# Layer two's output products in the last two passes: seven block products of 256 columns for eight of a half

## Chip, cores and metric

One core of a Trainium2 chip runs one program. The metric is the time of one execution in microseconds; of several runs the median is given. TensorE (PE in the rows) multiplies, VectorE (DVE), ScalarE (ACT) and GpSimd (POOL) do the element-wise work, SyncE (SP) issues nearly all transfers.

## What is computed

```python
def reference(**kwargs):
    ...
    attn_out = _attn_ref(**attn_kwargs)                    # q, k, v: (4, 8, 576, 64)
    x = np.ascontiguousarray(attn_out.transpose(0, 2, 1, 3)).reshape(B * S, H * D)
    x = _moe_ref(x=x, **moe_kwargs)                        # 512 -> 1536, gated -> 512
    return _moe2_ref(x=x, **moe2_kwargs)

def _moe2_ref(x, w_in, w_out):
    h = x @ w_in                                           # 2304x512 @ 512x2048
    r = np.maximum(h, 0.0)
    g = r * r
    return (g @ w_out).astype(np.float32)                  # 2304x2048 @ 2048x512
```

A causal retention with a decay per head comes first, then layer one, then layer two. The weights arrive as 64-bit floats and are rounded to 32-bit ones on the chip.

## The kernel before

**Numbers.** Every float32 operand of layers one and two is split into a high half and a low half of type fp32r (`split`: ScalarE copies the high half, VectorE subtracts it for the low one), and a product is three matmuls: high by high, high by low, low by high (`three`).

**Passes and systems.** Layer two runs in three passes (2,0), (2,1), (2,2) of 768 tokens, each token set in two halves a and b of 384. A pass has 8 systems; system k makes the hidden columns of two blocks of 128, for a and b. A system's input product is a 2x2 block product done with seven multiplications and sums (`slot`, products 1 to 7): a slot is 6 matmuls of 384 columns, into banks named g (two of them), v (two) and z (one). Evictions go to the tiles ca* (a) and cb* (b): ScalarE copies, VectorE adds and squares (`scalar_tensor_tensor`, the square of the positive part). The sums of the weights are made once, in pass (2,0), by GpSimd (`stationary`), and read back from DRAM as `wi` in later passes; the sums of the activations are renewed at the passes' borders (`renew`: xo_h, xo_l).

**Output products.** When the two blocks of a system are squared, `hidden` splits them into ho_hi and ho_lo. After every second system, `out2` multiplies them: for each half (a, b) and each 128 tokens j = 0, 1, 2 it makes a tile of 128 tokens by 512 output columns, in 4 blocks x 3 = 12 matmuls of 512 columns, the stationary operand being the 128x128 block of hidden values, the moving one a block of 128x512 of `wo` (high and low, loaded from DRAM by `load_out`). The tile is accumulated in one of three banks `a1` to `a3` (`out_bank`, named oacc) and added to `xy` by VectorE (in a pass's first pair of systems ScalarE copies it); after the last pair it is written out. `xy` holds the layer's inputs and, in the place of those used up, its outputs.

**Order.** The loop at the end runs over systems n: `seq` lists the slots, 1 and 2 and 6 and 5 of system n between 7 and 4 and 3 of system n - 1, with the output tiles of earlier systems (`outs`) and the loads (`fetch`) placed between them. A scheduler then fixes each engine's order from a timeline of its own; each engine takes its instructions strictly in that order.

**Memory.** Pools are stacked: raw and converted weights (`raw_p`, `cv_p`), then `ho2_p` and `wo2_p` for the second layer; on the other side `wi_p`, `s1_p`, `xs_p`, `xo_p` and `c4_p` (the tiles ca*, cb*).

## Time and profile before

| | |
|---|---|
| median of 3 runs | 875.48 us (874.52 to 876.61) |
| the profiled execution, first to last instruction | 875.1 us |
| TensorE busy | 863.9 us (99%), 5064 matmuls |
| weight loads on TensorE (beside matmuls) | 746.0 us (85%) |
| VectorE / ScalarE / GpSimd busy | 642.8 (73%) / 400.9 (46%) / 122.2 us (14%) |
| granted TensorE clock | full in all 40 slices |
| transfers | 203.62 MB, 65.8% of the queues' time |

The profile is one execution, and its span is the time that the working is made against; what lies around the span in a run is not shown. Matmuls overlap one another, so their durations add up to more than the time they take; the distance from one start to the next is what counts. Pass (2,1) begins near 605 us with the first slot of 384 columns of its first system; the last input product ends near 855 us, and only output products follow.

### The profile page before, as it was taken

How to read it: one execution, taken by the hardware profiler on the slowest of the kernel's cores; microseconds unless marked ns; L12 is line 12 of the kernel's file. 1: busy time of each engine (PE TensorE's matmuls, PEld its weight loads, DVE VectorE, ACT ScalarE, POOL GpSimd, SP SyncE). 2: the span in 40 equal slices, each digit the busy share in tenths (PEclk: the TensorE clock that was granted, in tenths of full speed). 3: DMA queues.
4: the chain of work that ended last, by engine and by line, in shares of the span. 5: the costliest groups of instructions: out<-in, count | busy, mean ns of one | idle time of the engine just before them, and what ended most of it. 6: DMA issues, size and time to landing. Idle time of an engine off the chain costs nothing.

```text
span 875.1 us, 13516 instructions
## 1 busy us (share of the span) xinstructions
PE 863.9 (99%) x5064; PEld 746.0 (85%) x5064; DVE 642.8 (73%) x1002; ACT 400.9 (46%) x709; POOL 122.2 (14%) x135
## 2 busy tenths in 40 slices
PE   9989999999999999999999999999999999999998
PEld 7878888888888888888888899989899988998987
DVE  3899999998976899677647999999534467533544
ACT  3657777565544544644325466554233233232310
POOL 3343343223130010000002311120000000000000
PEclk9999999999999999999999999999999999999999
DMA  9994777755554489878745388988666465656412
GB/s 337 402 356 160 253 249 249 264 186 211 196 192 154 139 282 379 297 273 288 253 141 185 144 315 328 361 304 313 206 239 215 126 226 210 190 202 204 164 41 73
DMA packets 75218, 203.62 MB, mean 233 GB/s; under 512 B 7696, under 2 KB 18448, under 8 KB 75152
## 3 DMA queue, kind: packets, MB, share of 16 engines
q1 hardware_dynamic: 74720, 202.34, 65.8%
q8 instruction: 40, 0.66, 0.3%
q10 hardware_dynamic: 432, 0.41, 0.1%
q14 instruction: 26, 0.21, 0.1%
HBM read 138.23 MB, written 64.49 MB: 232 GB/s over the span
## 4 chain that ended last, share of the span: by engine, by line
PE 86%; DVE 7%; DMA 4%; issue 2%; ACT 1%; SPq 0%; POOL 0%; DVEq 0%; POOLq 0%; ACTq 0%
PE oacc L113 42%; PE g L113 24%; PE v L113 12%; PE z L113 6%; DVE w L113 3%; DMA qk_sb<-in_qk 3%; DVE wi L113 1%; PE o L113 1%; DMA k_sb<-in_kv 1%; DMA qs_sb<-in_qscale 1%; PE s L113 1%; DVE xy L113 1%; DVE cbg L113 0%; PE kv L113 0%; DVE xo_l L113 0%
## 5 line engine op out<-in xcount | busy, mean ns | idle before, releaser
L113 PE MATMUL g<-xo_h,wi 128*128 128x384 f32 (+1 forms) x768 | 238.3, 364 | 0.0
L113 PE MATMUL oacc<-wo,ho_hi 128*128 128x512 f32 (+1 forms) x584 | 179.5, 388 | 0.0
L113 PEld LDWEIGHTS g<-xo_h,wi 128*128 128x128 f32 x768 | 142.5, 188 | 17.1
L113 PE MATMUL oacc<-ho_hi,wo 128*128 128x512 f32 (+1 forms) x480 | 151.1, 370 | 0.5 <-ACT xy L113 0.5
L113 DVE TENSOR_TENSOR xy<-oacc,xy 128x512 f32<-128x512 f32 (+1 forms) x155 | 99.6, 648 | 59.6 <-PE oacc L113 59.1
L113 PE MATMUL g<-xo_l,wi 128*128 128x384 f32 (+1 forms) x384 | 139.6, 364 | 0.0
L113 PEld LDWEIGHTS oacc<-wo,ho_hi 128*128 128x128 f32 x584 | 108.4, 188 | 19.2
L113 PE MATMUL v<-xo_h,wi 128*128 128x512 f32 (+1 forms) x384 | 123.2, 364 | 0.0
L113 PE MATMUL oacc<-wo,ho_lo 128*128 128x512 f32 (+1 forms) x292 | 113.3, 390 | 0.0
L113 PEld LDWEIGHTS oacc<-ho_hi,wo 128*128 128x128 f32 x480 | 88.1, 188 | 17.6 <-ACT xy L113 1.3
L113 PE MATMUL oacc<-ho_lo,wo 128*128 128x512 f32 (+1 forms) x240 | 89.1, 371 | 0.0
L113 PEld LDWEIGHTS g<-xo_l,wi 128*128 128x128 f32 x384 | 72.1, 188 | 8.4
L113 DVE TENSOR_SCALAR w<-w 128x512 f32<-128x512 f32 (+1 forms) x136 | 64.9, 480 | 18.0 <-ACT w L113 17.0
L113 PEld LDWEIGHTS v<-xo_h,wi 128*128 128x128 f32 x384 | 71.2, 188 | 8.0
L113 DVE TENSOR_TENSOR cbg<-v,cbg 128x384 f32<-128x384 f32 (+1 forms) x72 | 43.1, 598 | 45.8 <-ACT cbg L113 24.3
L113 ACT ACTIVATE cag<-g 128x384 f32<-128x384 f32 (+1 forms) x36 | 19.0, 528 | 125.2 <-PE g L113 125.1
L113 PE MATMUL v<-xo_l,wi 128*128 128x512 f32 (+1 forms) x192 | 69.8, 363 | 0.0
L113 PEld LDWEIGHTS oacc<-wo,ho_lo 128*128 128x128 f32 x292 | 54.8, 188 | 11.2
L113 PE MATMUL z<-xo_h,wi 128*128 128x512 f32 (+1 forms) x192 | 62.5, 365 | 0.0
L113 ACT CAST ho_hi<-cbg 128x768 fp32r<-128x768 f32 (+1 forms) x36 | 32.7, 908 | 45.5 <-DVE cbg L113 44.4
L113 DVE SCALAR_TENSOR_TENSOR w<-raw,w 128x512 uint32<-128x512 uint32 x68 | 52.5, 773 | 0.7
L113 PEld LDWEIGHTS oacc<-ho_lo,wo 128*128 128x128 f32 x240 | 45.1, 188 | 8.7
(90 smaller groups left out, 1295.6 us busy)
## 6 DMA issues: line engine op xcount, KB each, us to landing
wi<-win SPq DMA_DIRECT2D x84, 512.0 KB, 4.2
raw<-in_w SPq DMA_DIRECT2D x68, 512.0 KB, 4.9
win<-wi SPq DMA_DIRECT2D x60, 512.0 KB, 3.6
wo<-wsp SPq DMA_DIRECT2D x44, 512.0 KB, 6.4
wsp<-wo SPq DMA_DIRECT2D x28, 512.0 KB, 5.2
qk_sb<-in_qk SPq DMA_DIRECT2D x15, 576.0 KB, 7.4
wst<-w SPq DMA_DIRECT2D x32, 256.0 KB, 6.0
wi<-win SPq DMA_DIRECT2D x28, 256.0 KB, 5.4
```

What stands on the lines that cost most here:

```text
L113: i = op(*args, **kw)
```

## The change

In passes (2,1) and (2,2) the output products of a pair of systems become 2x2 block products with seven multiplications. A block row is a 128-token tile of a or of b (same j), a block column one of the two hidden blocks of a system, and the output columns are taken in halves of 256. A product is then 2 systems x 3 = 6 matmuls of 256 columns (`out3`). Each token pair j has seven of them, accumulated in two banks: 1, 6, 7, 4 in one and 5, 3, 2 in the other, and most of them are added to `xy` between two products of the same bank.

The operands: `block_tiles` gives ca* and cb* (now caa, cab) for both systems of a pair at once, in two sets of buffers. `sums2` has GpSimd make four sums of blocks per token pair, in the part of `xy` that pass (2,0) has left; `prepare` splits the seven operands of a token pair with three copies of 512, 256 and 1024 columns on ScalarE and as many subtractions on VectorE (hs_h, hs_l, two buffers). For the weights, `sums` has GpSimd make four sums of the raw blocks per system in pass (2,1) (w_o), which `operand2` splits (wt) and stores (tsp); pass (2,2) loads them from there; the three unsummed blocks are loaded from wsp. `hidden`'s splits, `load_out` and `out2` remain for pass (2,0) only. The products are taken from `stream` at 1.5 per slot from slot 23 on (`flow`).

```diff
@@ -54,6 +54,10 @@
+PRODUCTS = (1, 5, 6, 3, 7, 2, 4)
+START = 2
@@ -652,7 +661,10 @@
-        if i == 1:
+        if i == 1 and n >= turn_over:
+            s["x"] = bank("g")[:, :m]
+            s["a"], s["b"] = block_tiles(n)
+        elif i == 1:
@@ -707,6 +719,8 @@
     def hidden(n, which, c):
+        if n >= turn_over:
+            return
@@ -763,23 +777,115 @@
+    def block_tiles(n):
+
+        k = systems[n][2]
+        if k % 2 == 0:
+            home = block_pools[k // 2 % 2]
+            pairs_of[n] = pairs_of[n + 1] = [
+                home.tile([P, 2, 2, M[2]], F32, tag=f"g{x}", name=f"ca{x}") for x in "ab"
+            ]
+        return [x[:, k % 2] for x in pairs_of[n]]
...
+    def sums(n):
+
+        w0, w1_ = raw_o[n]
+        b11, b12, b21, b22 = (w[:, a:a + 256] for w in (w0, w1_) for a in (0, 256))
+        for a, x, y, op in ((b22, b22, b12, ALU.subtract), (b12, b12, b11, ALU.subtract),
+                            (b11, b11, b22, ALU.add), (b21, b21, b11, ALU.subtract)):
+            pool_e.tensor_tensor(out=a, in0=x, in1=y, op=op)
+
+    def operand2(n, i):
+
+        ph, p, k, what = systems[n]
+        w = moving[n, i] = t_p.tile([P, 2, 256], F32R, tag=f"t{i}", name="wt")
+        if i in (1, 2, 3):
+            f, at = {1: (0, 0), 2: (1, 0), 3: (1, 256)}[i]
+            sp.dma_start(out=w.bitcast(F32), in_=wsp[2, "o", 2 * k + f][:, :, at:at + 256])
+            return
+        x = (6, 5, 4, 7).index(i)
+        if p == 1:
+            split(w[:, 0], w[:, 1], raw_o[n][x // 2][:, x % 2 * 256:][:, :256])
+            sp.dma_start(out=tsp[k][:, x], in_=w.bitcast(F32))
+        else:
+            sp.dma_start(out=w.bitcast(F32), in_=tsp[k][:, x])
...
+    def sums2(n, j):
+
+        a, b = (x[:, :, :, j * P:(j + 1) * P] for x in pairs_of[n])
+        a11, a12, a21, a22 = (x[:, :, f] for x in (a, b) for f in range(2))
+        sums_of[n, j] = s = xy[:, :, 2 * P * j:2 * P * (j + 1)].rearrange("p i (s q) -> p i s q", q=P)
+        for x, y, z, op in ((0, a21, a22, ALU.add), (2, a11, a21, ALU.subtract),
+                            (1, s[:, 0], a11, ALU.subtract), (3, a12, s[:, 1], ALU.subtract)):
+            pool_e.tensor_tensor(out=s[:, x], in0=y, in1=z, op=op)
+
+    def prepare(n, j):
+
+        a, b = (x[:, :, :, j * P:(j + 1) * P] for x in pairs_of[n])
+        hi, lo = (hl_p.tile([P, 7, 2, P], F32R, tag=x, name=f"hs_{x}") for x in "hl")
+        halves[n, j] = hi, lo
+        split(hi[:, 0:2], lo[:, 0:2], a.rearrange("p s f q -> p f s q"))
+        split(hi[:, 2], lo[:, 2], b[:, :, 1])
+        split(hi[:, 3:7], lo[:, 3:7], sums_of[n, j])
...
+    def out3(n, j, at):
+
+        ph, p, k, what = systems[n]
+        i = PRODUCTS[at]
+        if at < 2:
+            banks[j, at] = out_bank()
+        o = banks[j, at % 2 if at < 6 else 0]
+        o = o[:, 256:] if i == 2 else o[:, :256]
+        x = (1, 2, 4, 5, 6, 7, 3).index(i)
+        for s in range(2):
+            hi, lo = (z[:, x, s] for z in halves[n, j])
+            th, tl = (moving[n - 1 + s, i][:, y] for y in range(2))
+            for y, (c, d) in enumerate(((hi, th), (hi, tl), (lo, th))):
+                pe.matmul(
+                    o, c, d, start=i in (1, 5, 2) and s + y == 0, stop=s == 1 and y == 2, skip_group_check=True
+                )
...
+        if k == 1 and i in (1, 5, 6, 4):
+            act.copy(home, src)
+        else:
+            tt(out=home, in0=src, in1=home, op=ALU.add)
+        if k == F2 // 2 - 1 and i in (3, 7, 2, 4):
+            half = slice(256 * half, 256 * half + 256)
+            sp.dma_start(out=out[t0:t0 + P, half].rearrange("p (c q) -> p c q", q=P), in_=home)
@@ -869,9 +975,91 @@
+    def follow(n, j, at):
+        out3(n, j, at)
+        own = [m for m in (n + 2, n + 3) if m < end]
+        if j == 2:
+            for m in own:
+                operand2(m, PRODUCTS[at])
+        if at == 6:
+            flowed["out"] += 1
+            ready_halves()
...
+            slots["n"] += 1
+            flow(int(1.5 * (slots["n"] - begin_at)))
...
+            t_p, hl_p = pool(ctx, "t_p", 3), pool(ctx, "hl_p", 2)
```

The rest of the diff moves pools (those of the raw weights, `ho2_p` and `wo2_p` are closed in pass (2,1) to make room for `t_p`, `hl_p` and the second set of ca*, cb*) and splits the last loop at system `turn_over`, the first of pass (2,1).

**Where the order moves.** First TensorE, at the first pair of systems of pass (2,1), behind the third product (bank v) of its second system. Before, an output tile of pass (2,0) follows at once:

```order
L113 MATMUL v_6494<-xo_l_6355,wi_6352 128x384
L113 MATMUL v_6494<-xo_h_6354,wi_6352 128x384 x2
L113 MATMUL v_6494<-xo_l_6355,wi_6352 128x384
L113 MATMUL v_6494<-xo_h_6354,wi_6352 128x384
L113 MATMUL oacc_6601<-wo_6097,ho_hi_6217 128x512 x2
L113 MATMUL oacc_6601<-wo_6097,ho_lo_6218 128x512
L113 MATMUL oacc_6601<-wo_6102,ho_hi_6217 128x512 x2
L113 MATMUL oacc_6601<-wo_6102,ho_lo_6218 128x512
L113 MATMUL oacc_6601<-wo_6240,ho_hi_6348 128x512 x2
L113 MATMUL oacc_6601<-wo_6240,ho_lo_6349 128x512
L113 MATMUL oacc_6601<-wo_6245,ho_hi_6348 128x512 x2
L113 MATMUL oacc_6601<-wo_6245,ho_lo_6349 128x512
```

Now 18 matmuls of input products, 12 block products on the plain blocks (oacc_6770 and oacc_6883) and 18 more of input products follow; then stands the piece below, whose oacc rows are the first on sums (hs_h_6716 is token pair 0, hs_h_6724 token pair 1):

```order
L120 MATMUL v_6841<-xo_h_6239,wi_6677 128x384
L120 MATMUL v_6841<-xo_l_6240,wi_6677 128x384
L120 MATMUL v_6841<-xo_h_6239,wi_6677 128x384 x2
L120 MATMUL v_6841<-xo_l_6240,wi_6677 128x384
L120 MATMUL v_6841<-xo_h_6239,wi_6677 128x384
L120 MATMUL oacc_6786<-wt_6576,hs_h_6716 128x256 x2
L120 MATMUL oacc_6770<-wt_6580,hs_h_6716 128x256 x2
L120 MATMUL oacc_6883<-wt_6580,hs_h_6724 128x256 x2
L120 MATMUL oacc_6786<-wt_6576,hs_l_6717 128x256
L120 MATMUL oacc_6786<-wt_6598,hs_h_6716 128x256 x2
L120 MATMUL oacc_6786<-wt_6598,hs_l_6717 128x256
L120 MATMUL oacc_6770<-wt_6580,hs_l_6717 128x256
```

Between the last matmul of that third product and the first of oacc_6786 stand 36 matmuls of 384 columns and 12 of 256. Output products start here after a pause in which only input products run.

Second, GpSimd. Before, its queue ends with the sums of the input weights of pass (2,0):

```order
L113 TENSOR_TENSOR w_in_5611<-w_in_5611 128x256 [waits Pool_49]
L113 TENSOR_TENSOR s1_5978<-w_in_5779 128x256 [waits DMAHW1_49,DVE_49]
L113 TENSOR_TENSOR w_in_5779<-w_in_5778,w_in_5779 128x256 [waits DMAHW7_49,Pool_49]
L113 TENSOR_TENSOR w_in_5778<-s1_5978,w_in_5778 128x256 [waits DVE_49,Pool_49]
L113 TENSOR_TENSOR w_in_5778<-w_in_5778 128x256 [waits Pool_49]
```

Now the sums of the first pair of systems follow (`sums2`; caa_6364 and cab_6365 are its a and b, xy_78 takes the sums). The first two sums of each of the three token pairs come first, then the third ones, a sum of weights (w_o) and the fourth ones:

```order
L120 TENSOR_TENSOR xy_78<-cab_6365 128x256 [waits DMAHW5_49,DMAHW4_49,DVE_49]
L120 TENSOR_TENSOR xy_78<-caa_6364,cab_6365 128x256
L120 TENSOR_TENSOR xy_78<-cab_6365 128x256 [waits DMAHW6_49,DMAHW0_49]
L120 TENSOR_TENSOR xy_78<-caa_6364,cab_6365 128x256
L120 TENSOR_TENSOR xy_78<-cab_6365 128x256 [waits DMAHW6_49,DMAHW1_49]
L120 TENSOR_TENSOR xy_78<-caa_6364,cab_6365 128x256
L120 TENSOR_TENSOR xy_78<-xy_78,caa_6364 128x256 [waits Pool_49] x3
L120 TENSOR_TENSOR w_o_6619<-w_o_6619,w_o_6618 128x256 [waits DMAHW4_49,DMAHW3_49,Activation_49]
L120 TENSOR_TENSOR xy_78<-caa_6364,xy_78 128x256 [waits Pool_49] x3
```

ScalarE's copy hs_h_6716<-xy_78 of 1024 columns waits for the first of the last three, which is the eleventh instruction of this piece.

Third, VectorE near the end, where no input products are left. Before, low halves are done ahead of the evictions:

```order
L113 SCALAR_TENSOR_TENSOR cbg_8095<-cbg_8095 128x2x384 [waits DVE_49]
L113 TENSOR_TENSOR ho_lo_8235<-cag_8094,ho_hi_8234 128x768 [waits Activation_49]
L113 TENSOR_TENSOR ho_lo_8261<-cbg_8095,ho_hi_8260 128x768 [waits Activation_49]
L113 TENSOR_TENSOR xy_78<-oacc_8278,xy_78 128x4x128 [waits PE_49]
L113 TENSOR_TENSOR xy_78<-oacc_8293,xy_78 128x4x128 [waits PE_49]
L113 TENSOR_TENSOR xy_78<-oacc_8308,xy_78 128x4x128 [waits PE_49]
L113 TENSOR_TENSOR xy_78<-oacc_8323,xy_78 128x4x128 [waits PE_49]
L113 TENSOR_TENSOR xy_78<-oacc_8338,xy_78 128x4x128 [waits PE_49]
L113 TENSOR_TENSOR xy_78<-oacc_8353,xy_78 128x2x128 [waits PE_49]
L113 TENSOR_TENSOR xy_78<-oacc_8368,xy_78 128x2x128 [waits PE_49]
```

Now each token pair's three subtractions (hs_l) stand among the evictions of the pair ahead; one round of it:

```order
L120 TENSOR_TENSOR hs_l_9137<-caa_8713,hs_h_9136 128x512 [waits Activation_49]
L120 TENSOR_TENSOR xy_78<-oacc_9154,xy_78 128x2x128 [waits PE_49]
L120 TENSOR_TENSOR hs_l_9137<-cab_8714,hs_h_9136 128x256 [waits Activation_49]
L120 TENSOR_TENSOR xy_78<-oacc_9144,xy_78 128x2x128 [waits DVE_49,PE_49]
L120 TENSOR_TENSOR hs_l_9137<-xy_78,hs_h_9136 128x1024 [waits Activation_49]
L120 TENSOR_TENSOR xy_78<-oacc_9217,xy_78 128x2x128 [waits PE_49]
L120 TENSOR_TENSOR xy_78<-oacc_9154,xy_78 128x2x128 [waits PE_49]
L120 TENSOR_TENSOR xy_78<-oacc_9144,xy_78 128x2x128 [waits PE_49]
L120 TENSOR_TENSOR xy_78<-oacc_9217,xy_78 128x2x128 [waits PE_49]
L120 TENSOR_TENSOR xy_78<-oacc_9154,xy_78 128x2x128 [waits PE_49]
```

The subtraction of 1024 columns has moved in front of the eviction of oacc_9217, whose bank TensorE needs three products later.

## Rows read from the trace of the kernel before

**Rows 1.** the page, busy time, share of the span and instructions of each engine

```profile
PE 863.9 (99%) x5064; PEld 746.0 (85%) x5064; DVE 642.8 (73%) x1002; ACT 400.9 (46%) x709; POOL 122.2 (14%) x135
```

**Rows 2.** windows: busy us (instructions) by engine; then TensorE's granted clock, DMA share, GB/s

```profile
480.00:520.00 40.00, 40.00 (x201) 36.06 (x200) 37.90 (x55) 20.44 (x36) 12.70 (x12) 1.00 0.56 203
605.00:872.00 267.00, 266.86 (x1336) 239.77 (x1334) 130.24 (x189) 71.41 (x119) 0.00 (x0) 1.00 0.54 180
```

**Rows 3.** timeline of TensorE, pass (2,1): start us, us, engine, line, op out<-in, shape, count

```profile
639.99 0.34 PE L113 MATMUL v<-xo_h,wi 128*128 128x384 f32 x1
...
643.12 0.63 PE L113 MATMUL oacc<-wo,ho_hi 128*128 128x512 f32 x2
...
645.89 0.34 PE L113 MATMUL z<-xo_h,wi 128*128 128x384 f32 x1
```

**Rows 4.** chain that ended last: start, us, what, count; then timeline of TensorE, end

```profile
854.67 17.21 PE oacc L113 x87
...
863.84 0.39 PE L113 MATMUL oacc<-wo,ho_lo 128*128 128x512 f32 x1
...
868.60 0.39 PE L113 MATMUL oacc<-wo,ho_lo 128*128 128x512 f32 x1
...
869.42 0.28 PE L113 MATMUL oacc<-wo,ho_lo 128*128 128x256 f32 x1
...
871.58 0.28 PE L113 MATMUL oacc<-wo,ho_lo 128*128 128x256 f32 x1
```

**Rows 5.** groups by form, VectorE, 605 to 872 us: busy us, mean ns | idle before

```profile
L113 DVE TENSOR_TENSOR cbg<-v,cbg 128x384 f32<-128x384 f32 x33 | 18.4, 557 | 34.4 <-ACT cbg L113 21.4 <-PE v L113 12.9
...
L113 DVE SCALAR_TENSOR_TENSOR cbg<-cbg 128x768 f32<-128x768 f32 x17 | 16.2, 953 | 0.0
...
L113 DVE TENSOR_TENSOR xy<-oacc,xy 128x256 f32<-128x256 f32 x2 | 0.8, 425 | 1.8 <-PE oacc L113 1.8
```

**Rows 6.** groups by form, whole run, VectorE (two rows) and ScalarE (three)

```profile
L113 DVE TENSOR_TENSOR ho_lo<-cbg,ho_hi 128x1024 fp32r<-128x1024 f32 x12 | 14.7, 1226 | 0.1
...
L113 DVE TENSOR_TENSOR wo<-wo 128x512 fp32r<-128x512 f32 x16 | 10.7, 681 | 0.2 <-ACT wo L113 0.2
...
L113 ACT CAST xo_h<-xy 128x1024 fp32r<-128x1024 f32 x14 | 14.5, 1049 | 12.6 <-DVE xy L113 4.1 <-PE g L113 4.1 <-PE z L113 3.5
...
L113 ACT CAST wi<-w_in 128x512 fp32r<-128x512 f32 x24 | 14.9, 620 | 17.3 <-DMA w_in<-wst 8.8 <-PE z L113 3.1 <-POOL w_in L113 2.8
...
L113 ACT CAST wi<-s 128x256 fp32r<-128x256 f32 x20 | 8.1, 407 | 6.6 <-POOL s L113 5.3 <-issue 0.6 <-POOL w_in L113 0.5
```

**Rows 7.** timeline of GpSimd, then of VectorE, pass (2,0)

```profile
562.20 0.74 POOL L113 TENSOR_TENSOR w_in<-w_in 128x256 f32<-128x256 f32 x1
563.02 1.34 POOL L113 TENSOR_TENSOR w_in<-s,w_in 128x256 f32<-128x256 f32 x1
...
562.67 1.08 DVE L113 TENSOR_TENSOR ho_lo<-cag,ho_hi 128x768 fp32r<-128x768 f32 x1
563.67 0.96 DVE L113 TENSOR_TENSOR wi<-s,wi 128x256 fp32r<-128x256 f32 x1
564.56 1.49 DVE L113 SCALAR_TENSOR_TENSOR cbg<-cbg 128x768 f32<-128x768 f32 x1
```

**Rows 8.** timeline: VectorE's last eviction; ScalarE's copy and the matmul behind it

```profile
871.90 0.42 DVE L113 TENSOR_TENSOR xy<-oacc,xy 128x256 f32<-128x256 f32 x1 [1.01 <-PE oacc L113]
...
61.27 0.58 ACT L113 COPY xy<-o 128x512 f32<-128x512 f32 x1
...
61.99 0.55 PE L113 MATMUL o<-qs,sb 64*64 64x128 f32 x6 [0.93 <-ACT xy L113]
```

**Rows 9.** DMA queues and issues, 605 to 872 us: count, KB each, median us to landing

```profile
q1 hardware_dynamic: 21989, 47.97, 53.4%
...
out<-xy SPq DMA_DIRECT2D x17, 256.0 KB, 2.7
wi<-win SPq DMA_DIRECT2D x14, 256.0 KB, 5.9
```

More of the change, by code (lines that the diff above doesn't have):

```diff
@@ L782, in retention_moe_kernel @@
-    flip = systems.index((2, 0, 0, "i"))
+        o = out_bank()
+        for r in range(4):
+            w = wos[2 * k - 2 + r]
+            h = [x[:, r % 2, j * P:(j + 1) * P] for x in hid[n - 1 + r // 2, which]]
+            three(o, h, (w[:, 0], w[:, 1]), r == 0, r == 3)
+        home = xy[:, :, t0:t0 + P]
+        src = o.rearrange("p (c q) -> p c q", q=P)
+        if k == 1:
+            act.copy(home, src)
+        else:
+            tt(out=home, in0=src, in1=home, op=ALU.add)
+        if k == F2 // 2 - 1:
+            sp.dma_start(out=out[t0:t0 + P].rearrange("p (c q) -> p c q", q=P), in_=home)
@@ new lines, in retention_moe_kernel, with fetch_raw @@
+    pairs_of, block_pools = {}, []
+    def block_tiles(n):
[6 more added lines that the diff above has]
+        return [x[:, k % 2] for x in pairs_of[n]]
+    moving, raw_o = {}, {}
+    tsp = [part_p.tile([P, 4, 2, 256], F32, tag=f"t{k}", name="tsp") for k in range(F2 // 2)]
+    def fetch_raw(n):
+        raw_o[n] = [xs_p.tile([P, 512], F32, tag="x", name="w_o") for x in range(2)]
+        for x, w in enumerate(raw_o[n]):
+            sp.dma_start(out=w, in_=wst[2, "o", 2 * systems[n][2] + x])
@@ L814, in retention_moe_kernel @@
     end = len(systems)
-    for n in range(end + 4):
+    for n in range(turn_over):
         ph, p, k, what = systems[n] if n < end else (0, None, 0, "")
@@ L871, in retention_moe_kernel, with ready_halves @@
             pass
-        if (ph, p) == (2, 0) and systems[n + 1][1]:
-            for _ in convert:
-                pass
+    for _ in convert:
+        pass
+    stream = [
+        (n, j, at) for n in range(turn_over + 1, end, 2) for j in range(3) for at in range(7)
+    ]
+    flowed, slots, queue, prepared = {"n": 0, "out": 0}, {"n": 0}, [], {"n": 0}
+    def ready_halves():
+        while queue and prepared["n"] < flowed["out"] + 2:
+            prepare(*queue.pop(0))
+            prepared["n"] += 1
@@ new lines, in follow @@
+    def follow(n, j, at):
[7 more added lines that the diff above has]
+            ready_halves()
+        raw = [m for m in own if systems[m][1] == 1]
+        if (j, at) == (0, 6):
+            for m in raw:
+                fetch_raw(m)
+        if (j, at) in ((1, 2), (1, 5)):
+            for m in raw[at // 5:][:1]:
+                sums(m)
@@ new lines, in flow @@
+    def flow(upto):
+        while flowed["n"] < min(upto, len(stream)):
+            follow(*stream[flowed["n"]])
+            flowed["n"] += 1
+    begin_at = 7 * 3 + START
+    for n in range(turn_over, end + 1):
+        tiles = outs.get(n, [])
+        seq = [(1, n), (7, n - 1), (2, n), (4, n - 1), (6, n), (3, n - 1), (5, n)]
+        if n == turn_over:
+            seq = [(7, n - 1), (4, n - 1), (3, n - 1), None, (1, n), (2, n), (5, n), (6, n)]
+        make = build(n + 1) if n + 1 < end else iter(())
+        for x in fetch.get((n, 0), []):
+            load_out(*x)
+        for x in seq:
+            if x is None:
+                blocks.close()
+                block_pools.append(pool(ctx, "ca_p", 1, side="right"))
+                fetch_raw(n)
+                fetch_raw(n + 1)
+                continue
+            i, k = x
+            if k == end:
+                continue
+            slot(k, i)
+            if i == 3 and k >= turn_over and systems[k][2] % 2:
+                for j in range(3):
+                    sums2(k, j)
+                    queue.append((k, j))
+                ready_halves()
+            next(make, None)
+            if tiles:
+                fn, *args = tiles.pop(0)
+                fn(*args)
+            slots["n"] += 1
+            flow(int(1.5 * (slots["n"] - begin_at)))
+            after(k, i)
+        for _ in make:
+            pass
+        if n == turn_over:
+            sums(n)
+            sums(n + 1)
+        if n == turn_over + 1:
+            second.close()
+            front.close()
+            t_p, hl_p = pool(ctx, "t_p", 3), pool(ctx, "hl_p", 2)
+            block_pools.append(pool(ctx, "cb_p", 1, side="right"))
+            for m in range(turn_over, turn_over + 3):
+                if m == turn_over + 2:
+                    fetch_raw(m)
+                    sums(m)
+                for i in PRODUCTS:
+                    operand2(m, i)
```

51 lines of the change are left out of this document (26 added, 25 removed).

## Prediction

> **What bounds the kernel now.** First the page's busy times: TensorE is busy for 99% of the span [rows 1]. Then the windows: from 605 us, where passes (2,1) and (2,2) begin, TensorE is busy for 266.86 of 267 us at the full granted clock (1.00, the 2.4 GHz level), while VectorE does 130 us and GpSimd nothing [rows 2]. In this stage, then, time is the number of TensorE's instructions times the pitch at which they start; a change pays if it lowers that sum and if nothing that it adds elsewhere makes TensorE wait.
>
> The pitch is read from start times in the timeline, not from durations, since matmuls overlap. From 639.99 to 643.12 stand 18 matmuls of 384 columns: 174 ns each. From 643.12 to 645.89 stand 12 of 512 columns: 231 ns [rows 3]. In the end stretch, which holds only output products, 21 steps of 512 columns lie between 863.84 and 868.60 (227 ns) and 18 steps of 256 columns between 869.42 and 871.58: 120 ns [rows 4]. A 256-column matmul thus costs 53% of a 512-column one, not half.
>
> **What is removed and added on TensorE.** Before, a pair of systems has 6 output tiles of 12 matmuls; 8 pairs give 576, of which the last tile is cut, so 564 of 512 columns and 24 of 256. The end stretch of 17.21 us holds 87 of them [rows 4], 63 being of 512 columns; the other 501 lie among input products. 501 x 231 + 63 x 227 + 24 x 120 ns = 132.9 us goes. Now a pair has 3 token pairs x 7 products x 6 matmuls of 256 columns: 1008 x 120 ns = 121.0 us comes. **Gain 11.9 us**; with 227 ns for all 564 it would be 9.8, the lower end. The Trainium skill (TensorE: Matmul & The Clock Gate, Back-to-back issue gap) gives a warm gap of columns / 2.4 + 2.5 ns, so 216 and 109 ns; by it the gain would be an estimated 14.4 us. The rows show a dearer small matmul, so I keep 11.9.
>
> **VectorE.** Instructions follow each other about 0.08 us before the recorded end of the one ahead (562.67 + 1.08 = 563.75 against 563.67 [rows 7]), which I take off each. Per system stay five instructions of 384 columns and one of 768: 5 x 0.48 + 0.87 = 3.3 us [rows 5], 52 us for 16. New: 144 evictions of 256 columns at 0.34 (49 us; 24 more go to ScalarE), 24 triples of low halves of 512, 256 and 1024 columns at 0.60 + 0.34 + 1.15 [rows 5, 6] (50 us), 32 subtractions of 256 for the weights (11 us). Ten instructions of 768 renew the inputs (9 us) and nine late evictions of pass (2,0) cost 5. Sum 176 us in the 255 us that are left: no bound by itself. Before, such a load did no harm: between 480 and 520 us VectorE was busy 37.9 of 40 us, GpSimd 12.7, and TensorE 40.00 [rows 2].
>
> **Where TensorE waits now.** Four places, each from the order.
>
> *Start of the block products.* The first product that needs sums (oacc_6786 with hs_h_6716) stands, by the order, 36 matmuls of 384 and 12 of 256 columns behind the last matmul of product 3 of the second system: 6.3 + 1.4 = 7.7 us, 7.9 from that matmul's start. What must happen in that time: TensorE to VectorE 0.32 (871.58 to 871.90 [rows 4, 8]), slightly more for 384 columns, say 0.4; the addition, 0.56; two low halves that the order puts ahead of the square, 2 x 0.60; the square, 0.95 [rows 5]. Then GpSimd: the copy of the sums waits for the eleventh instruction of its queue (six first sums of all three token pairs, three second ones, one of weights, then its own), since the queue takes all three pairs abreast. Pitch of such a sum: 562.20 to 563.02, 0.82 us [rows 7], so 9.0. Then the copy of 1024 columns, 1.05 [rows 6], and ScalarE to TensorE 0.14 (61.27 + 0.58 to 61.99 [rows 8]). Sum 13.3; **wait 13.3 - 7.9 = 5.4 us**, once. Nothing covers it: TensorE's queue is in order, and behind the waiting matmul stand input products. Lower end 2.9: sums that follow each other without the 0.08 us gap (0.74 each, -0.9), and low halves already done, -1.2, and a little from the handovers, -0.4. Upper end 12: all eleven sums stretched as the 1.34 us one [rows 7], +6.6. I take the middle since few VectorE instructions with two SBUF operands stand there. In the later pairs the same distance is 14 us or more, so they hide it.
>
> *Handing over halves.* hs_h and hs_l have two buffers: token pair t+2 is copied when pair t's last matmul is done. By the order, 10 of the 22 handovers leave no more than 13 matmuls of 256 columns or as much of others, 1.7 us from the last start to the first. The copy needs 0.32 + 0.62 + 0.14 = 1.1 us and is in time; the low half adds 0.68 [rows 6, 8] and is wanted 0.24 later: 1.8 against 1.9. An eviction ahead of it on VectorE (0.34) makes it late by some 0.2. I take 0.1 each, 1.0 us; ends 0 and 3.
>
> *The end.* After the last input product only output products are left, about 41, at 6 x 120 = 0.72 us. Per token pair VectorE has 7 x 0.34 + 2.09 = 4.47 us to do in 5.04. A bank is used again by the third product behind: 2.16 us from first matmul to first matmul, of which 0.60 + 0.32 + 0.42 + 0.14 = 1.48 go to the products and the eviction; 0.68 is left. The order puts the low half of 1024 columns (1.15) ahead of one of the evictions: 0.47 late, in five token pairs: 2.3 us; ends 0 and 5 (the next eviction late as well).
>
> *Transfers.* Weights now come as pieces of 256 KB per product, half the width: 128 issues of 256 KB more (w_o, wt, tsp both ways), 32 of 512 KB less, so 17 MB on top of what took 53.4% of the queues' time in the stage; about 73%. A piece has at least 4.8 us (40 matmuls of 256 columns) from the release of its buffer to its use, mostly 10; pieces of this size landed after 2.7 (quiet) and 5.9 us (among others) [rows 9]. I take 0.3; ends 0 and 3. SyncE's queue is in order, so a piece that waits for TensorE holds up the input weights behind it; these are asked for a system ahead (7 products and more) and stay hidden, or fall under the same 3 us.
>
> ScalarE gets 24 triples of 0.62 + 0.41 + 1.05 and is busy under half the time; the last eviction and transfer out are as before.
>
> **Sum.** 11.9 - 5.4 - 1.0 - 2.3 - 0.3 = 2.9 us. The profiled execution spans 875.1, so 872.2; the median of the runs, 875.48, lies 0.4 above that span, so 872.6.
>
> **Rivals.**
> *(a) The waits hide.* If the first sums are ready in time and the end runs smoothly, 11.9 less about 3 remains: 866.6, or 863.6 without any wait. For it: TensorE had not one visible gap in the stage before, under the same kind of generated order [rows 2]. Against: the eleven sums are counted, and their pitch was measured.
> *(b) VectorE and GpSimd take turns* (slower). GpSimd gets 128 sums, 128 x 0.74 = 95 us, where it had nothing. A VectorE subtraction of 256 columns beside one took 0.96 instead of some 0.42, a square of 768 columns 1.49 instead of 0.95 [rows 5, 7]. If each sum held VectorE up by its length, VectorE would need 176 + 95 = 271 us where TensorE needs 255, and the stage would last 4 longer than its 267: 879.5 us by the runs. It decides from 79 of the 95 us on. Against: evictions read PSUM, and the stretch in [rows 2]. The Trainium skill (SBUF — State Buffer, SBUF: two separate sides) calls the shared port pair an exclusive lock for VectorE instructions with two SBUF inputs and GpSimd ones; the stretched rows agree with it.
> *(c) The waits add up to their upper ends or near* (start 8, handovers 2, end 3, transfers 1): the 11.9 us go, 877.6 at most, 875 as a middle.
> A small matmul bound by its weight load (188 ns busy each) would cost 1008 x 68 ns more, 69 us; the 18 steps at 120 ns exclude it [rows 4].
>
> **How the numbers follow.** Chances: my forecast 0.50, (a) 0.20, (b) 0.14, (c) 0.16. The range for 8 in 10 reaches from 865.5, into (a), to 879.5, (b)'s own value. A measurement can tell 0.2% or 1.75 us from no change, so faster is below 873.7, slower above 877.2. Faster: (a) and four fifths of my forecast, 0.60; the same: a fifth of it and half of (c), 0.18, rounded up to 0.20 for waits between; slower: (b) and a part of (c), 0.20.
>
> **What would show it.** In the new profile: 1008 matmuls of 256 columns at 120 ns (wrong if above 125); one wait of TensorE of about 5 us at the first product on sums, released by ScalarE's copy behind GpSimd (wrong if under 2); short waits of some 0.4 us for VectorE at every token pair of the end; no wait for a transfer over 1 us. VectorE's busy share in the stage should rise to about 75%, and its two-operand instructions should be longer where GpSimd works; if TensorE's gaps there sum to over 8 us, (b) or (c) holds.

## The result, and the profile after

The changed kernel takes 887.07 us (median of 4 runs, 885.46 to 887.52) against 875.13 us before (median of 4 runs, 874.52 to 876.61), 11.9 us slower, where the forecast was 2.9 us faster and the range ended at 879.5. The ratio on record is 1.0129 (95% interval 1.0114 to 1.0143; the two medians by themselves give 1.0136). The two profiled executions span 885.2 and 875.1 us, 10.1 apart. A run takes 1.8 us more than its span (886.96 and 885.2 here, and the same in the runs of the kernel before), so the profiled execution before was some 1.7 above its median, which is the difference to 11.9.

The page of the changed kernel, busy times and the 40 slices of four rows, answering to [rows 1]:

```profile
PE 860.8 (97%) x5484; PEld 761.7 (86%) x5484; DVE 718.7 (81%) x1181; ACT 429.9 (49%) x793; POOL 231.3 (26%) x263
...
PE   8999999999999999999999999999979998999988
...
DVE  3899999998986998777658999898567998766786
...
POOL 3343243123220000000012230141086544412340
PEclk9999999999999999999999999999989999999999
```

TensorE has holes where it had none, and in one slice its granted clock falls. The windows of the stage and of parts of it, answering to [rows 2] (busy us and instructions of TensorE, its weight loads, VectorE, ScalarE, GpSimd; granted clock, DMA share, GB/s):

```profile
605.00:882.00 277.00, 262.39 (x1752) 253.80 (x1750) 207.48 (x371) 101.49 (x204) 103.64 (x120) 0.99 0.71 233
...
640.00:660.00 20.00, 15.10 (x83) 14.27 (x83) 13.91 (x18) 8.29 (x19) 16.36 (x18) 0.83 1.05 384
...
700.00:740.00 40.00, 34.69 (x228) 32.01 (x227) 38.34 (x62) 16.88 (x33) 26.49 (x27) 1.00 0.67 220
```

The averages of the stage are near the predicted ones: transfers 0.71 (73% predicted), VectorE busy for 207.5 us, 75% (about 75% predicted). Counted as the prediction counted, the durations of VectorE's 371 instructions add up to 227.9 us, or 198 after 0.08 us for each, where 176 had been summed; some 18 of the 22 more are instructions lengthened beside GpSimd (below). Inside it, the queues are full from 640 to 660 us and VectorE is busy for 38.3 of 40 us from 700 to 740. Who made TensorE wait (us, times, longest), first in the whole stage, then between 657 and 742 us alone:

```profile
PE oacc L120 <- DVE xy L120: 5.2, 10, 1.4
PE v L120 <- DMA wi<-win: 4.6, 1, 4.6
PE g L120 <- DMA wi<-win: 1.6, 1, 1.6
PE v L120 <- DVE cab L120: 1.3, 2, 1.0
PE oacc L120 <- DVE hs_l L120: 1.3, 3, 0.5
```

```profile
PE oacc L120 <- DVE xy L120: 2.5, 5, 1.1
PE g L120 <- DMA wi<-win: 1.6, 1, 1.6
PE v L120 <- DVE cab L120: 1.0, 1, 1.0
PE oacc L120 <- DVE hs_l L120: 0.2, 1, 0.2
```

Such waits understate the loss, since matmuls overlap. In the table below, "lost" is the sum of what each distance between two starts of matmuls has beyond the pitch (0.174 us for 384 columns, 0.230 for 512, 0.119 for 256); before, it is zero from 605 us on. The last column says about how much of the sum fell while the granted clock stood at 0.50 (the 1.2 GHz level), which it did once or twice in each of these executions but those of e6 and e10.

| kernel | median us | lost 640–657 | 657–742 | 742–840 | 840 to end | sum | at half clock |
|---|---|---|---|---|---|---|---|
| changed | 887.1 | 7.4 | 8.4 | 1.9 | 5.0 | 22.8 | 1.8 |
| e1 sums by pair | 886.7 | 3.8 | 10.4 | 3.0 | 5.0 | 22.1 | 1.5 |
| e2 third system later | 886.8 | 3.7 | 10.8 | 1.9 | 5.0 | 21.4 | 1.5 |
| e3 both | 883.6 | 2.3 | 10.4 | 2.3 | 4.9 | 19.9 | 3.0 |
| e4 short sums | 882.2 | 6.9 | 5.0 | 0.6 | 3.6 | 16.1 | 2.1 |
| e5 tail split | 889.7 | 7.2 | 8.7 | 1.9 | 7.5 | 25.3 | 2.9 |
| e6 = e3 + squares on ScalarE | 877.4 | 2.8 | 5.0 | 0.9 | 3.8 | 12.4 | 0.0 |
| e7 = e6 + sums on VectorE | 881.9 | 4.7 | 7.8 | 0.7 | 4.6 | 17.9 | 4.1 |
| e8 = e6 + tail on GpSimd | 876.8 | 2.0 | 7.8 | 1.1 | 3.8 | 14.8 | 1.5 |
| e9 = e8 + stores later | 878.5 | 0.0 | 8.3 | 1.0 | 4.0 | 13.4 | 1.3 |
| **e10 = e9 + slot 25** | **872.0** | 0.0 | 3.8 | 2.3 | 3.3 | 9.4 | 0.0 |
| e11 changed, slot 25 | 884.1 | 7.1 | 7.0 | 1.7 | 4.6 | 20.4 | 2.0 |
| e12 = e9 + slot 27 | 881.5 | 0.0 | 5.7 | 0.8 | 9.9 | 16.3 | 2.8 |
| e13 = e9 + slot 29 | 891.9 | 0.0 | 12.6 | 10.0 | 8.1 | 30.8 | 3.8 |

The times are medians of 4 to 10 runs, the losses those of one profiled execution each, which need not be the median one: e6's ten runs took 875.4 to 877.0 us where the mean granted clock was 1.000 and 876.8 to 880.9 where it was lower, and the profiled one is of the first kind. For the change itself the losses close: from the first of the last 672 matmuls of 384 columns (16 systems x 7 x 6, the input products of the two passes) to the last matmul's start 266.1 us pass before and 276.8 after, and 266.1 - 11.9 + 22.8 = 277.0. So the gain on TensorE came as worked out, and the waits are 22.8 us where 9.0 had been summed.

**The start.** TensorE of the changed kernel (start us, us, engine, line, op, shape, count):

```profile
639.82 0.33 PE L120 MATMUL v<-xo_h,wi 128*128 128x384 f32 x1
...
647.31 0.33 PE L120 MATMUL v<-xo_h,wi 128*128 128x384 f32 x1
652.22 0.69 PE L120 MATMUL v<-xo_h,wi 128*128 128x384 f32 x1 [4.58 <-DMA wi<-win]
652.70 0.52 PE L120 MATMUL v<-xo_l,wi 128*128 128x384 f32 x1
...
654.30 1.48 PE L120 MATMUL oacc<-wt,hs_h 128*128 128x256 f32 x6
...
659.91 0.40 PE L120 MATMUL oacc<-wt,hs_h 128*128 128x256 f32 x2
...
661.34 0.34 PE L120 MATMUL g<-xo_h,wi 128*128 128x384 f32 x1
```

SyncE's queue and ScalarE's copy of the first sums:

```profile
630.63 1.37 SPq L120 DMA_DIRECT2D wi<-win  x2
632.05 1.24 SPq L120 DMA_DIRECT2D wt<-wsp  x2
...
644.47 1.83 SPq L120 DMA_DIRECT2D wt<-wsp  x3
646.52 3.28 SPq L120 DMA_DIRECT2D wi<-win  x5
```

```profile
651.94 2.00 ACT L120 CAST hs_h<-xy 128x1024 fp32r<-128x1024 f32 x2 [0.28 <-POOL xy L120]
```

Twelve matmuls of 256 columns lie between 659.91 and 661.34: 119 ns each, 120 predicted from [rows 4]. From the last matmul of the third product (639.82) to the end of the first copy of 1024 columns (651.94 + 1.05) and 0.14 more are 13.3 us: the predicted chain, to the tenth. But TensorE never got to wait for it. Between 632.05 and 646.52 SyncE issued twenty pieces (wt, tsp, w_o and one output) and no wi; the wi of the next input product landed at 652.2, 4.7 us late, just ahead of that place, which TensorE so reached at 654.30 with the sums ready, and the matmuls behind it ran at half speed, 0.32 us each, until 656.2 us (granted clock 0.50 from 652.2 to 656.2).

### The profile page after: what moved, and what is told of

It reads as the page before. It is cut to its first block, busy times and chain, and to the rows that moved or that the text cites. A ratio compares the mean times of both kernels' runs of the same rounds, so it can differ in the third digit from the quotient of the medians.

```text
span 885.2 us, 15055 instructions
## 1 busy us (share of the span) xinstructions
PE 860.8 (97%) x5484; PEld 761.7 (86%) x5484; DVE 718.7 (81%) x1181; ACT 429.9 (49%) x793; POOL 231.3 (26%) x263
## 4 chain that ended last, share of the span: by engine, by line
PE 79%; DVE 7%; DMA 7%; POOL 3%; ACT 2%; issue 1%; SPq 0%; ACTq 0%; DVEq 0%; POOLq 0%
PE oacc L120 36%; PE g L120 23%; PE v L120 11%; PE z L120 6%; DMA k_sb<-in_kv 3%; POOL xy L120 2%; DVE hs_l L120 2%; PE o L120 2%; DMA w_o<-wst 1%; DVE w L120 1%; DMA qk_sb<-in_qk 1%; DVE xy L120 1%; PE s L120 1%; PE kv L120 1%; DVE cab L120 1%
## 5 line engine op out<-in xcount | busy, mean ns | idle before, releaser
L120 PE MATMUL g<-xo_h,wi 128*128 128x384 f32 (+1 forms) x768 | 241.6, 364 | 1.6 <-DMA wi<-win 1.6
L120 DVE TENSOR_TENSOR xy<-oacc,xy 128x256 f32<-128x256 f32 (+1 forms) x262 | 132.5, 516 | 55.2 <-PE oacc L120 54.5
L120 PE MATMUL oacc<-wt,hs_h 128*128 128x256 f32 x672 | 125.9, 286 | 5.6 <-DVE xy L120 5.2
L120 PE MATMUL v<-xo_h,wi 128*128 128x512 f32 (+1 forms) x384 | 125.3, 368 | 5.9 <-DMA wi<-win 4.6
L120 PEld LDWEIGHTS oacc<-wt,hs_h 128*128 128x128 f32 x672 | 107.5, 191 | 8.7 <-DVE xy L120 5.7
L120 PE MATMUL oacc<-wt,hs_l 128*128 128x256 f32 x336 | 94.1, 284 | 1.3 <-DVE hs_l L120 1.3
L120 PEld LDWEIGHTS v<-xo_h,wi 128*128 128x128 f32 x384 | 71.6, 189 | 14.8 <-DMA wi<-win 4.9
L120 PEld LDWEIGHTS oacc<-wt,hs_l 128*128 128x128 f32 x336 | 63.4, 190 | 2.3 <-DVE hs_l L120 2.1
L120 PE MATMUL oacc<-wo,ho_hi 128*128 128x512 f32 x192 | 60.1, 391 | 0.0
L120 POOL TENSOR_TENSOR xy<-cab 128x256 f32<-128x256 f32 x24 | 19.9, 830 | 135.1 <-DVE cab L120 125.1
L120 ACT ACTIVATE raw<-raw 128x512 uint32<-128x512 uint16 x68 | 46.0, 676 | 14.6 <-DMA raw<-in_w 14.5
```

The source lines that it names most:

```text
L120: i = op(*args, **kw)
```

## Experiments

**e1 to e3: the start, its two late things apart.** e1 takes the sums pair by pair (the line of sums2: GpSimd's next sums stand behind those of the pair before), e2 puts the third system's weights off (the other two pieces), e3 is both.

```diff
 def sums2(n, j):
...
+    pool_e.last = pool_e.recent
...
-for m in range(turn_over, turn_over + 3):
-    if m == turn_over + 2:
-        fetch_raw(m)
-        sums(m)
+for m in range(turn_over, turn_over + 2):
...
 def follow(n, j, at):
...
+    if n == turn_over + 1 and (j, at) == (0, 2):
+        fetch_raw(n + 1)
+        sums(n + 1)
+        for i in PRODUCTS:
+            operand2(n + 1, i)
```

> One part changed: GpSimd takes the sums of hidden blocks token pair by token pair instead of all three abreast, so that those of token pair 0 are ready about 6 us earlier (their fourth sum at about 646 instead of 652 us). Theory A (at the start of the block products two things were late at once, the input weights wi, which stand behind a burst of twenty pieces in SyncE's queue, and the sums; each hides the other): no gain, within 1.5 us of the changed kernel's 887.1, and TensorE still waits 4 to 5 us for wi near 647. Theory B (the sums alone set the start, as predicted; the late wi is an accident): 4 to 5 us faster, 882 to 883.

> One part changed: the output weights of the third system of pass (2,1), wanted only by the second pair of systems, are fetched, summed, split and stored after the third block product instead of ahead of the first: in SyncE's queue the first late input weights (wi, 256 KB) then stand 15 instead of 20 issues behind the first piece of the block products. Theory A (two things late at once): the wait for wi near 647 us falls below 1 us, TensorE instead waits some 4 us at the first product on sums, which are ready at about 652 to 653 us as before; 1 to 3 us faster than the changed kernel (884 to 886). Theory C (the transfers are short of bandwidth for long, not only in a burst): the wait for wi moves to the next input weights, over 3 us in sum, and the time stays within 1 us.

> Both parts: sums token pair by token pair, and the third system's output weights later. Theory A: the 7.2 us that TensorE lost from 645 to 657 us fall to under 1.5, so 5 to 7 us faster than the changed kernel, 880 to 882. Theory B (sums alone): no better than the kernel with the sums alone. Theory C (bandwidth): under 2 us better than the changed kernel.

Measured: 886.66, 886.83 and 883.60 us. At the place itself e3 came near what theory A said: its start loses 2.3 instead of 7.4 us (under 1.5 had been said), the wait for wi is 1.0. But the time gains 3.5, not 5 to 7: of the 5.1 us gained, 2.0 are lost again between 657 and 742. e1 and e2 lose 3.6 and 3.7 us less at the start and 1.9 and 2.4 more behind it, and e1 another 1.0 after 742. A good part of what comes back is the clock: between 657 and 742 the granted clock fell to half twice in e3 (about 3.0 us of the 10.4), once each in e1 and e2 (1.5 of 10.4 and of 10.8), and not at all in the changed kernel, which had its half-clock stretch at the start. Without it e3's border loses 7.4 us, less than the changed kernel's 8.4, and e1's and e2's 8.9 and 9.3. At the start e1 went against all three theories: SyncE's queue was as full, but with other sums the scheduler put twenty matmuls of block products (652.75 to 657.6 us in e1's trace) ahead of the late input slot, which so began at 658.01 without a wait for wi; in its place stand waits of 0.5 us for a piece of weights and 0.3, 0.9 and 0.95 us for hs_h, hs_l and an eviction. e2 showed no wait for sums of the length that A foresaw. So theory B falls with e1's time, C with e3's start, and A was half of it: what stands behind the start sets the rest.

**e4: GpSimd's sums an eighth as wide.**

```diff
-pool_e.tensor_tensor(out=s[:, x], in0=y, in1=z, op=op)
+q = 16 if systems[n][1:3] in ((1, 5), (1, 7), (2, 1), (2, 3), (2, 5), (2, 7)) else P
+pool_e.tensor_tensor(out=s[:, x, :, :q], in0=y[:, :, :q], in1=z[:, :, :q], op=op)
```

> In the last two pairs of systems of pass (2,1) and in all of pass (2,2), the sums of hidden blocks are made for 16 of each 128 tokens only, so that GpSimd's instructions there get an eighth as wide; seven eighths of these sums are left out. The order of TensorE, VectorE, ScalarE and SyncE is the same, row for row. Theory D (VectorE is too slow from 696 to 732 us because GpSimd's sums stretch its instructions with two SBUF operands): these instructions fall back to their shortest (1024 columns 1.21 us, 768 columns 0.94, 256 columns 0.41), VectorE gets idle time between 696 and 732, the 6.65 us that TensorE lost from 712 to 742 fall below 3; 4 to 7 us faster than the changed kernel, 880 to 883. Theory E (VectorE has too many instructions of its own at the border of the passes, renewals and low halves together): it stays busy without a break, and under 2.5 us are gained. The 2.2 us lost after 855 us, where GpSimd does nothing, stay in both.

Measured: 882.23 us, 4.8 better. Four of VectorE's groups between 696 and 742 us (busy us, mean ns | idle), first in the changed kernel, then in e4:

```profile
L120 DVE TENSOR_TENSOR xo_l<-xy,xo_h 128x768 fp32r<-128x768 f32 x7 | 8.3, 1190 | 0.0
...
L120 DVE TENSOR_TENSOR wt<-w_o,wt 128x256 fp32r<-128x256 f32 x8 | 4.7, 592 | 0.0
L120 DVE TENSOR_TENSOR xy<-xy 128x768 f32<-128x768 f32 x3 | 3.9, 1304 | 0.0
...
L120 DVE TENSOR_TENSOR hs_l<-cab,hs_h 128x256 fp32r<-128x256 f32 x4 | 2.7, 685 | 0.0
```

```profile
L120 DVE TENSOR_TENSOR xo_l<-xy,xo_h 128x768 fp32r<-128x768 f32 x7 | 6.7, 962 | 0.0
...
L120 DVE TENSOR_TENSOR wt<-w_o,wt 128x256 fp32r<-128x256 f32 x8 | 3.2, 413 | 0.0
L120 DVE TENSOR_TENSOR xy<-xy 128x768 f32<-128x768 f32 x3 | 2.9, 963 | 0.0
...
L120 DVE TENSOR_TENSOR hs_l<-cab,hs_h 128x256 fp32r<-128x256 f32 x4 | 2.2, 554 | 0.0
```

The same instructions in the same order are up to 43% longer beside full sums. Evictions, which read PSUM, are not (412 and 418 ns). The loss of 657 to 742 falls from 8.4 to 5.0, although 1.2 of the 5.0 are at half clock, and that of 742 to 840 from 1.9 to 0.6. From 712 to 742, where theory D wanted under 3 us, 6.65 become 3.7, one wait of 0.6 for a piece of weights among it: D holds for about half of what is lost there. The windows from 696 to 732, changed kernel and e4, show what is left of E:

```profile
696.00:732.00 36.00, 32.23 (x210) 30.27 (x208) 35.97 (x57) 17.10 (x32) 20.74 (x19) 1.00 0.74 244
```

```profile
696.00:732.00 36.00, 34.50 (x231) 33.37 (x230) 34.38 (x63) 17.59 (x33) 15.32 (x23) 1.00 0.80 276
```

In the changed kernel VectorE stood still for 0.03 us in 36, and in e4 it is at 95% (34.38) even so.

**e5: the large subtraction of the end cut in two.** The kernel that ran cuts it in the last two pairs of systems, six token pairs; the text on record says the last pair.

```diff
+if n >= end - 3:
+    split(hi[:, 3:5], lo[:, 3:5], sums_of[n, j][:, 0:2])
+    split(hi[:, 5:7], lo[:, 5:7], sums_of[n, j][:, 2:4])
+    return
 split(hi[:, 3:7], lo[:, 3:7], sums_of[n, j])
```

> One part changed: in the last pair of systems the copy and the subtraction of 1024 columns are made as two of 512 each. If, as predicted, the short waits of the end come from the eviction that stands behind the subtraction of 1024 columns (1.22 us) on VectorE, they go where the subtraction is split, for an eviction now stands between the two halves: 0.44 us each at three token pairs, 1.3 us in all; the wait of 1.6 us at the first token pair of the end (near 852 us) shrinks by no more than 0.5, for there both halves stand behind each other. If VectorE is simply too slow for output products alone (7 evictions and the low halves against 5.04 us of TensorE), the waits stay and only move. Time 885.5 or within 1 us of it; the trace decides.

Measured: 889.70 us, 2.6 slower. One token pair of the end, changed kernel and e5:

```profile
870.30 0.28 PE L120 MATMUL oacc<-wt,hs_l 128*128 128x256 f32 x1
870.86 0.47 PE L120 MATMUL oacc<-wt,hs_h 128*128 128x256 f32 x2 [0.28 <-DVE xy L120]
```

```profile
870.27 0.28 PE L120 MATMUL oacc<-wt,hs_l 128*128 128x256 f32 x1
870.59 0.50 PE L120 MATMUL oacc<-wt,hs_h 128*128 128x256 f32 x2
...
871.29 0.28 PE L120 MATMUL oacc<-wt,hs_l 128*128 128x256 f32 x1
871.62 0.47 PE L120 MATMUL oacc<-wt,hs_h 128*128 128x256 f32 x2
```

One distance of 0.56 us became two of 0.32 and 0.33, each 0.2 beyond the pitch: the wait only moved. The place of one subtraction was not its cause; all low halves of a token pair (2.1 us) stand in three gaps between evictions, and that together they overrun the slack is argued from this. The first token pair of the end lost 1.8 us more than in the changed kernel: there the two halves follow each other and take 2.36 us (at 849.56) where the whole took 1.76 (at 851.21), TensorE waits 2.03 instead of 1.44 us, and behind that wait the granted clock is at half from 852.0 to 855.4 us, 1.3 us more.

**e6 and e7: VectorE's own work less, then more.** e6 is e3 with the squares of passes (2,1) and (2,2) on ScalarE; e7 in addition makes the sums of hidden blocks on VectorE (the last two lines). The half a[:, 0] is treated as b is; a[:, 1] has its Relu on ScalarE already.

```diff
+elif n >= turn_over:
+    act.activation(out=b, in_=b, func=AF.Relu)
+    act.activation(out=b, in_=b, func=AF.Square)
 else:
     dve.scalar_tensor_tensor(out=b, in0=b, in1=b, **relu2)
...
-pool_e.tensor_tensor(out=s[:, x], in0=y, in1=z, op=op)
+dve.tensor_tensor(out=s[:, x], in0=y, in1=z, op=op)
```

> On top of the kernel with both parts (883.6 us): in passes (2,1) and (2,2) the squares of the positive part are made on ScalarE (the positive part, then its square) instead of VectorE, which takes some 2 us of 3.3 per system, 4.1 per pair of systems, off VectorE and puts 6 us per pair on ScalarE. Theory F (what is lost around the border of the passes is lost because VectorE has more to do than time passes): VectorE has idle time between 690 and 735 us, and the waits of TensorE from 675 to 742 us fall from 10.4 to 3 to 5; 5 to 8 us faster, 876 to 879. Theory G (the waits come from the order, in which some 17 output products follow each other behind the border, not from VectorE's sum): the waits stay above 8, under 2 us are gained.

> On top of the squares on ScalarE: the sums of hidden blocks (96 instructions of 256 columns with two SBUF operands) are made by VectorE instead of GpSimd; only the sums of the weights stay with GpSimd. VectorE gets 96 x 0.34 = 33 us of own work in the stage, and loses what GpSimd's sums add to its instructions. Theory D (the stretching is what hurts): no VectorE instruction is stretched outside the sums of weights, the first sums are ready 5 us earlier, and the time is that of the squares on ScalarE or up to 3 us better. Theory F (VectorE's own sum decides): VectorE's load is back where it was, and the time is 2 to 5 us worse than with the squares on ScalarE alone.

Measured: 877.39 us (6.2 better than e3) and 881.90 us (4.5 worse than e6). Between 657 and 742 us e6 waits for VectorE alone:

```profile
PE oacc L120 <- DVE xy L120: 2.3, 2, 1.9
PE oacc L120 <- DVE hs_l L120: 0.9, 1, 0.9
```

Both times are what theory F said, and theory G falls with e6. That less of VectorE's work gives the border back is shown at the place: 10.4 become 5.0 us, or 7.4 become 5.0 without e3's half clock. That more takes it away is shown by the time alone: e7's border loses 7.8 us, but 2.5 of them at half clock, so that 5.3 are left beside e6's 5.0, and 1.5 of what it loses more at the start is at half clock too. At an equal mean granted clock (0.996) e7's runs took 880.4 and 880.9 us and e6's 877.8 to 879.0, still 1.4 to 3.1 us apart. So D's stretching is not the whole, for e7 has none of it from the hidden sums and is slower; how the loss divides between stretching and VectorE's own work stays open.

**e8 to e10: towards a faster kernel.** Each holds the one before. e8, in prepare, shares the tail's large low half with GpSimd; e9 issues the stores of the first two systems' weights later, at place (0, 2) of the first pair; e10 lets a pair's output products begin two slots later (slot 21 + START, so 25 for 23).

```diff
+if n == end - 1 or (n, j) == (end - 3, 2):
+    act.copy(hi[:, 3:7], sums_of[n, j])
+    for e, q in ((dve, 0), (pool_e, 2)):
+        e.tensor_tensor(out=lo[:, 3 + q:5 + q], in0=sums_of[n, j][:, q:q + 2],
+                        in1=f32(hi[:, 3 + q:5 + q]), op=ALU.subtract)
...
-sp.dma_start(out=tsp[k][:, x], in_=w.bitcast(F32))
+stores.append((tsp[k][:, x], w.bitcast(F32)))
...
-START = 2
+START = 4
```

> On top of the squares on ScalarE (877.4 us), in the last four token pairs one half of the subtraction of 1024 columns goes to GpSimd, which is idle there; the order of TensorE, ScalarE and SyncE is the same row for row. Theory H (in the end VectorE's low halves of a token pair, some 2.1 us, stand in three gaps behind each other and overrun the 0.68 us of slack, wherever the large one is cut): with 0.5 us less of it the waits of about 0.44 us per token pair fall under 0.2, 1 to 2 us faster. Theory I (the port that VectorE and GpSimd share makes it no better): VectorE's other subtractions grow by as much and the waits stay.

> On top of that, the eight stores of split weights (256 KB each) of the first two systems are issued behind the third block product instead of ahead of the first. If the burst of transfers is what is left at the start, the wait for wi near 646 us (1.5 us) goes and the start loses under 1 us: 1 to 2 us faster than the kernel with the tail on GpSimd, 873 to 875. If the lateness is only handed on to VectorE's border, the time stays within 1 us.

> As before, and the block products start two input slots later (slot 25 instead of 23). The start has 2 us more lead for the sums and the weights, and three more output products are left for the end, where a token pair (7 products) loses at most 0.44 us. If the start is still late, 0 to 2 us faster than with slot 23; if the border of the passes sets the time, for VectorE has the same work there, no change within 1 us or slower.

e8, 876.83 us: the end loses 3.8 as in e6. VectorE and GpSimd there:

```profile
859.72 1.29 POOL L120 TENSOR_TENSOR hs_l<-xy,hs_h 128x512 fp32r<-128x512 f32 x1 [2.18 <-ACT hs_h L120]
...
860.02 1.55 DVE L120 TENSOR_TENSOR hs_l<-xy,hs_h 128x512 fp32r<-128x512 f32 x1
```

VectorE's half took 1.55 us beside GpSimd's, longer than the whole of 1024 columns alone (1.22), as theory I has it. That holds for the two token pairs where the halves ran side by side (1.55 and 1.58 us; they lose 0.81 and 0.85 us, 0.44 each in e6). In the two others GpSimd came to its half only after VectorE, whose half took 0.89 us, and they lose 0.42 and 0.38 where e6 lost 0.87 and 0.83: less of the low halves on VectorE does help there, and the two effects cancel.

e9, 878.46 us, where 873 to 875 had been expected, or no change within 1 us: the start loses nothing any more, and the border 8.3 us (7.8 in e8), 6.3 of it after 700 us with one wait of 1.8 for a piece of weights among it. That the lateness is only handed on is not shown: the profiled execution of e9 is the fastest of its ten runs (875.95), that of e8 one of its slower ones (878.55), so their losses (13.4 and 14.8) stand the other way round from the medians, and the runs of the two overlap (875.95 to 880.52, 875.35 to 881.46).

e10, 872.01 us, 6.4 better than e9, where at most 2 had been expected: with two slots more of lead the border loses 3.8 us, 0.8 of it after 700 us, and the mean granted clock is 1.000 in all four runs (in one of ten of e9's). That is 0.9953 of before (0.9937 to 0.9969), the fastest kernel here. Its waits up to 742 us:

```profile
PE oacc L120 <- DVE hs_l L120: 1.3, 1, 1.3
PE z L120 <- DVE caa L120: 0.7, 1, 0.7
PE oacc L120 <- DMA wt<-wsp: 0.4, 1, 0.4
```

**e11 to e13: the lead alone, and more of it.** Only START differs: 4 in the changed kernel, 6 and 8 in e10's. With 6, the sums of the last pair of systems take the place of one token pair's of the pair before ahead of their split, with 8 at every pair, so that products work on other values with the same instructions.

> The changed kernel with nothing but the start of the block products two input slots later (slot 25 instead of 23). Theory J (each late chain needs its own cure: the burst of weights at the start, VectorE's and GpSimd's work at the border): the start loses about 2 us less, as it has 2 us more lead, the border loses what it lost (8 to 10 us from 657 to 742), and the time is 884 to 887. Theory K (the lead alone was too short, and with two slots more everything falls into place, as it did when the other parts were in): 4 us faster or more, below 883.

> The fastest kernel so far (872.0 us) with the start at slot 27 instead of 25. What is left there from 605 us on are some 9.4 us of waits, of which 2.7 between 675 and 700 us and about 4 in the end. If lead is still what lacks at the border, 1 to 2 us faster; if not, the same within 1 us, or slower by some 0.1 us for each product more in the end.

> The same with slot 29. If lead helps still, faster than with slot 27; if the products that are put off pile up at the border or in the end, 1 to 3 us slower than the best.

Measured: 884.14, 881.45 and 891.87 us. The lead alone gives 2.9 us (theory J by the time), but leaves the start at 7.1, where J had 2 us less. More lead is worse than expected: with slot 27 the end loses 9.9 us (2.8 at half clock), and with slot 29 the waits come everywhere, 6.6 us of them for weights (wt from tsp). Where the best slot lies is thus a matter of this order, and not settled.

## Why the prediction was wrong

In the sum, 9.0 us of waits had been priced and 22.8 came: 2.0 more at the start (7.4, nearly all for a late transfer and the clock behind it, in place of 5.4 for the sums), 6.6 for VectorE at the border of the passes, which had no term, 1.8 for a transfer there (0.3 had been priced for all of them), 0.9 more at the handovers and 2.7 in the end. No rival had as much: (b) came to some 16 us (11.9 and 4), (c) to 14 (8 + 2 + 3 + 1).

- **TensorE's gain** was right: 119 ns per matmul of 256 columns, and the sum closes within 0.2 us with 11.9 (its lower end, with 227 ns for all 564, comes to 9.9, not 9.8). The 109 ns by the formula that the Trainium skill (TensorE: Matmul & The Clock Gate, Back-to-back issue gap) gives for an isolated matmul are 10 ns too short for this stream.
- **VectorE: the step that failed.** "Sum 176 us in the 255 us that are left: no bound by itself" divided by the whole stage. Ten of the instructions that renew the inputs, eight of the weights' splits and the last pair's low halves fall into some 36 us at the border of passes (2,1) and (2,2), where VectorE had no pause (busy for 35.97 of 36 us); nothing was summed for that place, and of the 8.4 us lost between 657 and 742 it cost 6.6 (the other 1.8 are a transfer's). The load itself was 198 us, not 176: the lengthening beside GpSimd stood only in a rival, and 13 instructions of 768 columns renew the inputs where ten had been counted. The stretch of 480 to 520 us that I took as proof of harmlessness [rows 2] had VectorE at 95% too, but evictions there had no slack as short as 0.68 us behind them. That difference is argued, not tried.
- **Rival (b)** named the right engine, with too large a price and no place. Between 605 and 886 us the mean durations of VectorE's two-operand instructions are longer than undisturbed ones [rows 5 to 7] by 18 us in all (24 x 0.10, 24 x 0.11 and 24 x 0.16 of the low halves, 32 x 0.15 of weights, the rest renewals and squares) beside 104 us of GpSimd, not 95; far under the 79 from which it was to decide. At the border it counted all the same, for there VectorE had nothing to spare: with the short sums of e4 about half of the loss there goes. The Trainium skill (SBUF — State Buffer, SBUF: two separate sides) speaks of an exclusive lock of the shared port pair; e8's 1.55 us agrees.
- **Transfers, 0.3 (0 to 3): mis-sized.** Here too the average was right and the place wrong. That the input weights "are asked for a system ahead (7 products and more) and stay hidden, or fall under the same 3 us" failed: in SyncE's queue they stood behind the burst. With the clock behind it that wait cost 6.9 of the start's 7.4 us (4.7 the wait, some 1.8 the half clock, which the sum did not have; 0.5 of the 7.4 was a wait for VectorE's cab), and 1.8 more came with a wait that ended at 704.2 us.
- **Start, 5.4:** the chain was right at 13.3 us, but covered by the late wi. Two causes at one place do not add; taking away one alone (e1, e2) gained 0.4 and 0.2 us in the time, and both 3.5 (e3).
- **Handovers, 1.0:** 1.9 between 742 and 840 us, of which GpSimd's stretching is 1.3 (e4).
- **The end, 2.3:** the last four token pairs lose 0.44 to 0.50 us each where 0.47 had been worked out, at the eviction behind the large subtraction, as said; but e5 shows that an eviction put between its halves saves nothing: the place was right, and that this order alone costs the time was not. 2.7 more were lost at the first token pair of the end (848 to 856 us), where GpSimd still works and the large subtraction took 1.76 us, not 1.22.

## What to carry to other kernels

An engine's or a queue's load must be set against the time of the place where the work falls, windows of some 20 to 40 us at starts and borders, and not of the stage; average shares of 71 and 75% hid full queues for 20 us and a full VectorE for 36. When the engine that bounds is given less to do, price what is moved to the others at the borders first, and count a part of GpSimd's work on SBUF as time of VectorE (here 18 us for 104). And a gain at one place is not yet one in the time: of e3's 5.1 us at the start, 2.0 were gone 50 to 90 us later, where waits close together brought the granted clock to half.
